# The k-v products of a linear attention, two heads at once or each head in its own 64 columns of the array

## The chip, the cores and the metric

The kernel runs on one core of one Trainium2 chip. The core has a matrix engine (TensorE, PE in the profile, with its weight loads shown apart as PEld), a vector engine (VectorE, DVE), a scalar engine (ScalarE, ACT), GpSimd (POOL), and SyncE (SP), which here only issues transfers. The metric is device time in microseconds for one execution; less is better. Three runs of the kernel before took 1629.92, 1631.16 and 1631.63 us, so its time is 1631.16 us (median).

## The reference

Inputs are q, k and v of shape (8, 8, 576, 64): batch, heads, sequence, head dimension, all float32. Then come two MLPs on 4608 tokens with 512 features and 2048 hidden units.

```
q_s = exp(q - max(q, -1)) / (sum over the head dimension + 1e-9)
k_s = exp(k - max(k, 2))  / (sum over the sequence + 1e-9)
kv  = einsum('bhsd,bhse->bhde', k_s, v)         # 64 x 64 for each head
x   = einsum('bhsd,bhde->bhse', q_s, kv)        # -> 4608 x 512
h = x @ w_in1;  g = max(0.01 h, h);     x = g @ w_out1
h = x @ w_in2;  g = h * sigmoid(h);     out = g @ w_out2
```

The change concerns the third line alone, the product of k_s and v over the 576 tokens of a sequence. The kernel multiplies exp(k) with v and with a column of ones, so that the same product gives the sum of exp(k) that k_s is divided by.

## The kernel before, in words

The work is cut into units: one unit is a pair of heads of one batch element for k and v, and a pair of heads of one block of 512 tokens for q. There are 36 units for q (9 blocks, 4 pairs) and 32 for k and v (8 batch elements, 4 pairs). Three generators do a unit: `k_task` (maximum over the sequence, exp, the kv product, scaling), `v_task` (the transfers of v) and `q_task` (softmax of q, its transposes, the product with kv).

For kv, the 576 tokens of the two heads lie in six sets of tiles that are used in turn. The first 512 tokens lie on 128 partitions, four to a partition (four chunks c), the last 64 on 64 partitions, as a fifth chunk. A chunk of exp(k) is 128 partitions x 128 columns (64 of each head); a chunk of v is 128 x 129: 64 columns of each head and a column of ones (`NV = 2 * D + 1`). Line 508 multiplies four chunks, line 509 the fifth, which has only 64 partitions; all five add up in one PSUM tile `pk`, 128 x 129. Only its two 64 x 64 diagonal blocks are kv of a head; the two other blocks mix the heads and are not read. On float32 operands the program's one matmul is two weight loads and two matmuls on the engine, so a unit's five matmuls are ten loads and ten passes.

Line 515 adds 1e-9 to the sum that stands in column 128 of `pk`, line 516 takes its reciprocal, and line 521 scales the two diagonal blocks into a zeroed 128 x 128 tile (`kvbuf`), which line 623 uses as weights for the product with q.

The order of the work of all engines is written out by a planner (`Queues`) from costs and ranks: the kv products of a unit are one step there, `op(("p", 1.1))`. In the stretch of the kv products PE otherwise does the first layer of the first MLP (lines 651 to 653: three products of split operands, 512 columns each), the transposes of k maxima and q (480, 486, 608) and line 623. The kv products are spread over the first 361 us; after that come the rest of layer one and the three other layers (lines 872 and 922). SP issues the transfers in one queue, in the planner's order. Before the first unit, POOL writes the columns of ones (line 980) and zeroes `kvbuf` (line 982).

Of the kernel before, what the change touches and what calls it, by code (L numbers as in the profile page):

```python
# [13 lines left out]
ACTF = mybir.ActivationFunctionType  # L14
# [12 lines left out]
def v_tt(n):  # L27
    return 0.16 + n / 960
# [6 lines left out]
def a_(n):  # L35
    return 0.19 + n / 1200
# [14 lines left out]
def op(*engines):  # L51
    return "op", engines


def wait(*keys):
    return "wait", keys


def get(ring):
    return "get", ring  # L60


class Queues:
# [14 lines left out]
    def spawn(self, rank, gen):  # L78
        self.tasks.append([rank, next(self.count), self.now, gen, None, 0.0, None])
        self.tasks.sort(key=lambda t: t[:2])  # L80
        self.step(next(t for t in self.tasks if t[3] is gen), None)
# [8 lines left out]
    def done(self, key):  # L90
        self.events[key] = self.now
# [111 lines left out]
def linear_attention_two_mlps(  # L203
# [24 lines left out]
    nc = tc.nc  # L228
    B, H, S, D = q.shape
    NT, DM = out.shape  # L230
    DFF = w_in1.shape[1]
    P = 128
# [6 lines left out]
    SR = S - SM  # L239
    EPS = 1e-9  # L240
# [21 lines left out]
    gd = [tc.dram_tile([NG, 4, P, TB], F32, name=f"gd{j}") for j in range(NB)]  # L262

    NKV = 8
    NV = 2 * D + 1
    ident = const.tile([P, P], F32, name="ident")
    ones = const.tile([P, 1], F32, name="ones")
    kvbuf = [const.tile([P, P], F32, name=f"kv{i}") for i in range(NKV)]
# [35 lines left out]
    def w_room(n, shape, dt, name):  # L304

        return wp.tile(shape, dt, tag=f"s{n}", name=f"{name}{n}")
# [43 lines left out]
    def split1(f):  # L350

        room = NW - NF + f
        raw = w_room(room, [P, 2 * DM], U32, "rw")
        yield from load_bits(raw, 0, 0, f)
        t = yield get(r_o)
        yield from decode(raw, t, DM)
        w = w_room(room, [P, 2, DM], F32R, "w")
        wtiles[f] = w
        yield op(("A", a_(DM)))
        copy("A", w[:, 0], t)  # L360
        yield op(("V", v_tt(DM)))
        sub("V", w[:, 1], t, w[:, 0])
        r_o.put(t)
        done(("w", f))
# [70 lines left out]
    sets = []  # L435
    for n in range(6):
        k_, v_ = (w_room(2 * n + i, [P, 2 * DM], F32, "u") for i in range(2))
        sets.append((k_[:, 0:640], v_[:, 0:5 * NV]))
    r_kv = Slots(qs, sets)
    r_q = Slots(qs)  # L440
    for n in range(3):
        t = gp.tile([P, 2, TB], F32, tag=f"g{n}", name=f"uq{n}")
        r_q.add(t[:, 0], t[:, 1])

    def k_task(n):

        b, j, p = units[n]
        if n >= NU:
            yield wait(("kvs", n - NU))
        of[n] = yield get(r_kv)  # L450
        kf, vv = of[n]
        done(("set", n))
        heads = slice(2 * p, 2 * p + 2)

        yield op(("D", 0.73))
        nc.sync.dma_start(
            out=kf[:, 0:512].rearrange("p (h c) -> p h c", h=2),
            in_=k[b, heads, 0:SM, :].rearrange("h (p c) d -> p h (c d)", c=4),
        )
        kh = kf[:, 0:512].rearrange("p (h c d) -> p h c d", c=4, h=2)  # L460
        k4 = kf[:, 0:512].rearrange("p (h c d) -> p c h d", c=4, h=2)
        yield op(("D", 0.56))
        k1 = kf[0:SR, 512:640]
        nc.sync.dma_start(
            out=k1.rearrange("p (h d) -> p h d", h=2), in_=k[b, heads, SM:S, :].rearrange("h p d -> p h d")
        )
        m1 = yield get(r_m)
        m2 = yield get(r_o)
        m2v = m2[:, 0:4 * D].rearrange("p (h c d) -> p h c d", h=2, c=2)
        yield op(("V", v_tt(256)))  # L470
        nc.vector.tensor_tensor(out=m2v, in0=kh[:, :, 0:2], in1=kh[:, :, 2:4], op=ALU.max)
        yield op(("V", v_tt(128)))
        nc.vector.tensor_tensor(out=m1, in0=m2v[:, :, 0], in1=m2v[:, :, 1], op=ALU.max)
        r_o.put(m2)
        m1f = m1.rearrange("p h d -> p (h d)")
        yield op(("V", v_tt(128)))
        nc.vector.tensor_tensor(out=m1f[0:SR], in0=m1f[0:SR], in1=k1, op=ALU.max)
        pm = yield get(r_attn)
        yield op(("p", 0.12))
        nc.tensor.transpose(pm[:, 0:P], m1f, ident)  # L480
        r_m.put(m1)
        nm = small[n % NU]["k"][:, 0:1]
        yield op(("V", v_tt(128)))
        nc.vector.tensor_reduce(out=nm, in_=pm[:, 0:P], axis=AX.X, op=ALU.max, negate=True)
        yield op(("p", 0.12))
        nc.tensor.transpose(pm[:, P:2 * P], nm.to_broadcast([P, P]), ident)
        nb = pm[:, P:2 * P]
        yield op(("V", v_tt(512)))
        nc.vector.tensor_tensor(
            out=k4, in0=k4,  # L490
            in1=nb.rearrange("p (h d) -> p h d", h=2).unsqueeze(1).to_broadcast([P, 4, 2, D]), op=ALU.add,
        )
        yield op(("V", v_tt(128)))
        nc.vector.tensor_tensor(out=k1, in0=k1, in1=nb[0:SR], op=ALU.add)
        r_attn.put(pm)
        kx = yield get(r_kx)
        yield op(("A", a_(512)))
        nc.scalar.activation(
            out=kx.rearrange("p (c h d) -> p c h d", c=4, h=2), in_=k4, func=ACTF.Exp
        )  # L500
        yield op(("A", a_(128)))
        nc.scalar.activation(out=k1, in_=k1, func=ACTF.Exp)
        yield wait(("v", n), *([("xm", n - NKV + NP)] if n >= NKV - NP else []))
        vv = vv.rearrange("p (c n) -> p c n", c=5)
        pk = yield get(r_attn)
        yield op(("p", 1.1))
        for c in range(4):
            nc.tensor.matmul(pk[:, 0:NV], lhsT=kx[:, c * P:(c + 1) * P], rhs=vv[:, c, :], start=c == 0, stop=False)  # L508
        nc.tensor.matmul(pk[:, 0:NV], lhsT=k1, rhs=vv[0:SR, 4, :], start=False, stop=True)  # L509
        r_kv.put(of.pop(n))  # L510
        r_kx.put(kx)
        done(("kv", n))
        rk = small[n % NU]["k"][:, 1:2]
        yield op(("V", 0.15))
        nc.vector.tensor_scalar_add(rk, pk[:, 2 * D:NV], EPS)
        nc.vector.reciprocal(out=rk, in_=rk)
        w = kvbuf[(b * NP + p) % NKV]
        for i in range(2):
            o = slice(i * D, (i + 1) * D)
            yield op(("A", a_(64)))  # L520
            nc.scalar.activation(out=w[o, o], in_=pk[o, o], func=ACTF.Copy, scale=rk[o])
        kv[b, p] = w
        r_attn.put(pk)
        done(("kvs", n))

    def v_task(n):
        b, j, p = units[n]
        yield wait(("set", n))
        t = of[n][1]
        t = t.rearrange("p (c n) -> p c n", c=5)  # L530
        for i in range(2):
            yield op(("D", 0.73))
            nc.sync.dma_start(
                out=t[:, 0:4, i * D:(i + 1) * D],
                in_=v[b, 2 * p + i, 0:SM, :].rearrange("(p c) d -> p c d", c=4),
            )

            yield wait()
        yield op(("D", 0.56))
        nc.sync.dma_start(  # L540
            out=t[0:SR, 4, 0:2 * D].rearrange("p (h d) -> p h d", h=2),
            in_=v[b, 2 * p:2 * p + 2, SM:S, :].rearrange("h p d -> p h d"),
        )
        yield wait()
        done(("v", n))
# [423 lines left out]
    def step(j, f):  # L969
        return place[j, f]  # L970
# [4 lines left out]
    with tc.manual_schedule():  # L975
        nc.vector.memset(ones, 1.0)
        make_identity(nc, ident)
        nc.scalar.activation(out=small[0]["k"][:, 0:1], in_=ones, func=ACTF.Exp)
        for _, t in sets:
            nc.gpsimd.memset(t.rearrange("p (c n) -> p c n", c=5)[:, :, 2 * D:], 1.0)  # L980
        for t in kvbuf:
            nc.gpsimd.memset(t, 0.0)

        for n in range(NP):
            r = -40 + 5 * n
            spawn(r, k_task(n))
            spawn(r + 1, q_task(n))
            spawn(r + 5, v_task(n))
        for n in range(NP, len(units)):
            b, j, p = units[n]  # L990
            r = -12 + 3 * p if j == 1 else step(j, 0) - 14 + 4 * p
            if b is not None:
                spawn(r, k_task(n))
                spawn(r, v_task(n))
            spawn(r, q_task(n))
        for f in range(NF):
            spawn(-36 + 6 * f if f < 4 else step(0, f) - 4, split1(f))
            if f < NH:
                spawn(f, layer0(0, f))
        spawn(0, layer0_all())  # L1000
        for t in (convert1, convert2, convert3):
            spawn(1000, t())
        spawn(0, later())
        for i in range(NG):
            for l in (1, 2, 3):
                spawn(step2(l, 0, i) - 8, weights(l, i))
        spawn(step2(1, 0, 0) - 4, g_all(1))
        spawn(step2(2, 0, 0) - 5, x_all())
        spawn(step2(3, 0, 0) - 4, g_all(3))
        spawn(step2(1, 0, 0), layers())  # L1010
        qs.run()
# [30 lines left out]
```

## Time and profile before

| | |
|---|---|
| median of three runs | 1631.16 us |
| the profiled execution | 1635.08 us |
| its span, first to last instruction | 1633.1 us |
| PE busy | 1603.1 us, 98% |
| PEld busy | 1501.8 us, 92% |
| DVE / ACT / POOL busy | 1194.2 / 851.3 / 39.1 us |
| share of L508 and L509 in PE's busy time | 37.1 + 16.4 us |
| mean granted TensorE clock | 0.995 |

The profile counts a matmul as busy from when it starts to when its last result is out, and the next one starts before that, so the busy times of a run of matmuls overlap. How long a pass holds the engine is read from the distance of two starts, not from its own duration. In a row of the timeline the first number is a start, the second the time from there to the end of the last instruction of the row, and x8 says that eight instructions are merged.

### The profile page before, as it was taken

What the parts mean: (1) busy time and instruction counts of PE and PEld (TensorE: products, weight loads), DVE (VectorE), ACT (ScalarE), POOL (GpSimd) and SP (SyncE); (2) the same over time, 40 slices, a digit from 0 to 9 for tenths busy, and PEclk for the clock granted to TensorE, in tenths of its full rate; (3) what the DMA queues carried; (4) which work ended last, traced back from release to release, by engine and by line L of the source; (5) the groups of instructions that cost most, each with busy time, mean ns of one, the idle gap of its engine ahead of it and who ended that gap; (6) DMA issues with size and microseconds to landing.
All of it is one profiled execution on the core that took longest, in us unless ns stands there. A gap on an engine that the chain in (4) does not pass through costs nothing.

```text
span 1633.1 us, 30896 instructions
## 1 busy us (share of the span) xinstructions
PE 1603.1 (98%) x11456; PEld 1501.8 (92%) x11456; DVE 1194.2 (73%) x2205; ACT 851.3 (52%) x1824; POOL 39.1 (2%) x53
## 2 busy tenths in 40 slices
PE   6899999999999999999999999999999999999999
PEld 4688888888788999999999999999999999999999
DVE  8886656657566887777788966666669877777775
ACT  5768756766445544444447433444446544444442
POOL 2101001000000000000000000000000000000000
PEclk9899999999999999999999999999999999999999
DMA  8766767777779655454558344333338544444442
GB/s 227 234 195 167 209 196 240 212 242 230 225 235 311 214 150 168 141 170 145 166 143 277 131 152 140 131 133 133 135 130 279 163 131 135 133 130 136 134 132 78
DMA packets 251030, 287.25 MB, mean 176 GB/s; under 512 B 59392, under 2 KB 182272, under 8 KB 250880
## 3 DMA queue, kind: packets, MB, share of 16 engines
q1 hardware_dynamic: 250880, 285.29, 56.6%
q8 instruction: 90, 1.47, 0.4%
q14 instruction: 60, 0.49, 0.1%
HBM read 168.82 MB, written 116.39 MB: 175 GB/s over the span
## 4 chain that ended last, share of the span: by engine, by line
PE 93%; DVE 5%; DMA 1%; issue 0%; ACT 0%; SPq 0%; DVEq 0%; ACTq 0%
PE b L922 22%; PE h L922 21%; PE b L872 11%; PE h L872 11%; PE h L651 8%; PE h L653 8%; PE h L652 8%; PE a L623 2%; PE a L508 2%; PE a L608 1%; DVE o L810 1%; PE a L509 1%; DVE a L292 1%; DVE x L292 1%; DVE g L292 0%
## 5 line engine op out<-in xcount | busy, mean ns | idle before, releaser
L651 PE MATMUL h<-x,w 128*128 128x512 f32 x576 | 238.5, 414 | 2.3 <-ACT w L296 1.6
L296 ACT ACTIVATE x<-x 128x512 fp32r<-128x512 f32 x209 | 131.8, 631 | 205.8 <-DMA x<-gda 91.0
L653 PE MATMUL h<-x,w 128*128 128x512 f32 x576 | 225.9, 392 | 1.2 <-DVE w L292 1.2
L652 PE MATMUL h<-x,w 128*128 128x512 f32 x576 | 225.4, 391 | 0.8 <-DVE x L292 0.5
L810 DVE TENSOR_TENSOR o<-o,b 128x512 f32<-128x512 f32 x190 | 128.1, 685 | 72.5 <-PE b L872 39.7
L810 DVE TENSOR_TENSOR o<-o,h 128x512 f32<-128x512 f32 x188 | 126.6, 685 | 62.7 <-PE h L872 36.7
L884 ACT ACTIVATE o<-o 128x512 f32<-128x512 f32 x144 | 89.2, 629 | 145.5 <-DVE o L810 144.7
L684 ACT ACTIVATE o<-h 128x512 f32<-128x512 f32 x144 | 85.9, 597 | 118.0 <-PE h L653 109.0
L296 ACT ACTIVATE x<-o 128x512 fp32r<-128x512 f32 x169 | 105.2, 631 | 70.0 <-DVE o L810 53.8
L922 PE MATMUL b<-a,x 128*128 128x256 f32 x1080 | 141.4, 283 | 0.1
L292 DVE TENSOR_TENSOR x<-x 128x512 fp32r<-128x512 f32 x209 | 137.2, 684 | 2.5
L651 PEld LDWEIGHTS h<-x,w 128*128 128x128 f32 x576 | 108.8, 189 | 29.2 <-ACT w L296 2.5
L922 PEld LDWEIGHTS b<-a,x 128*128 128x128 f32 x1080 | 134.7, 192 | 0.3 <-DVE x L292 0.3
L922 PE MATMUL b<-x,a 128*128 128x256 f32 x1044 | 132.0, 284 | 0.6 <-DVE x L292 0.5
L653 PEld LDWEIGHTS h<-x,w 128*128 128x128 f32 x576 | 108.4, 188 | 25.6 <-DVE w L292 2.3
L872 PE MATMUL h<-x,a 128*128 128x256 f32 x1008 | 130.0, 283 | 1.3 <-DVE x L292 1.3
L652 PEld LDWEIGHTS h<-x,w 128*128 128x128 f32 x576 | 108.9, 189 | 22.8 <-issue 1.2
L922 PEld LDWEIGHTS b<-x,a 128*128 128x128 f32 x1044 | 128.1, 192 | 1.1 <-DVE x L292 1.0
L872 PEld LDWEIGHTS h<-x,a 128*128 128x128 f32 x1008 | 124.9, 192 | 1.5 <-DVE x L292 1.5
L922 PE MATMUL h<-x,a 128*128 128x256 f32 x996 | 126.0, 283 | 0.2
L872 PE MATMUL b<-x,a 128*128 128x256 f32 x960 | 123.8, 283 | 1.3 <-DVE x L292 1.3
L922 PEld LDWEIGHTS h<-x,a 128*128 128x128 f32 x996 | 122.3, 192 | 0.7 <-DVE x L292 0.6
(116 smaller groups left out, 2819.3 us busy)
## 6 DMA issues: line engine op xcount, KB each, us to landing
gda<-o SPq DMA_DIRECT2D x144, 256.0 KB, 2.6
gd<-o SPq DMA_DIRECT2D x144, 256.0 KB, 2.6
x<-gd SPq DMA_DIRECT2D x102, 256.0 KB, 2.7
x<-gda SPq DMA_DIRECT2D x89, 256.0 KB, 2.8
a<-wc SPq DMA_DIRECT2D x84, 256.0 KB, 4.3
wc<-o SPq DMA_DIRECT2D x72, 256.0 KB, 3.2
raw<-in_moe_w_out_dram SPq DMA_DIRECT2D x32, 512.0 KB, 4.2
g<-gda SPq DMA_DIRECT2D x37, 256.0 KB, 2.7
```

The costliest lines, as they stand in the source:

```text
L292: engines[e].tensor_tensor(out=out_, in0=a, in1=b.bitcast(F32), op=ALU.subtract)
L296: nc.scalar.activation(out=out_, in_=in_, func=ACTF.Copy)
L508: nc.tensor.matmul(pk[:, 0:NV], lhsT=kx[:, c * P:(c + 1) * P], rhs=vv[:, c, :], start=c == 0, stop=False)
L623: nc.tensor.matmul(po, lhsT=kv[bb, p], rhs=qT.rearrange("p (c t) -> p c t", c=4)[:, :, a:e], start=True, stop=True)
L651: nc.tensor.matmul(h, lhsT=w[:, 0, kk], rhs=x[:, 0], start=kk == 0, stop=False)
L652: nc.tensor.matmul(h, lhsT=w[:, 0, kk], rhs=x[:, 1], start=False, stop=False)
L653: nc.tensor.matmul(h, lhsT=w[:, 1, kk], rhs=x[:, 0], start=False, stop=kk == KD - 1)
L684: nc.scalar.activation(out=o, in_=h, func=ACTF.Prelu, alpha=0.01)
L810: nc.vector.tensor_tensor(out=o, in0=a, in1=b, op=alu)
L872: nc.tensor.matmul(bank[:, r * HB:(r + 1) * HB], lhsT=w4[:, a, r, k], rhs=x3[:, b, k], start=n == 0, stop=n == 5,)
L884: nc.scalar.activation(out=t, in_=t, func=ACTF.Silu)
L922: nc.tensor.matmul(bank[:, m * HB:(m + 1) * HB], lhsT=s[:, a, at:at + P], rhs=x[:, b, r * HB:(r + 1) * HB], start=i + m + n == 0, stop=i = ...
```

## The change

Each of the five chunks is multiplied head by head: the weights are the 64 columns of exp(k) of one head, the moving operand the 64 columns of v of that head and a column of ones of its own (65), and the result goes to that head's 64 partitions of `pk`, columns 0 to 64. So five matmuls of 128 x 129 become ten of 64 x 65, and the built program marks them as 128 x 64 parts of the array, at columns 0 and 64 in turn. The mixed blocks are no longer computed. The fifth chunk now has 128 partitions, the upper 64 of them zero in both k and v; POOL writes these zeros once, at the start. Three transfers of v have other destinations, the sum is read from column 64, and line 521 reads columns 0 to 63 for both heads.

```
-    NV = 2 * D + 1
+    NV = 2 * (D + 1)
...
-        for c in range(4):
-            nc.tensor.matmul(pk[:, 0:NV], lhsT=kx[:, c * P:(c + 1) * P], rhs=vv[:, c, :], start=c == 0, stop=False)
-        nc.tensor.matmul(pk[:, 0:NV], lhsT=k1, rhs=vv[0:SR, 4, :], start=False, stop=True)
+        for c in range(5):
+            kc = kx[:, c * P:(c + 1) * P] if c < 4 else kf[:, 512:640]
+            for h in range(2):
+                o = slice(h * D, (h + 1) * D)
+                nc.tensor.matmul(
+                    pk[o, 0:D + 1], lhsT=kc[:, o], rhs=vv[:, c, h * (D + 1):(h + 1) * (D + 1)],
+                    start=c == 0, stop=c == 4,
+                )
...
-        nc.vector.tensor_scalar_add(rk, pk[:, 2 * D:NV], EPS)
+        nc.vector.tensor_scalar_add(rk, pk[:, D:D + 1], EPS)
...
-            nc.scalar.activation(out=w[o, o], in_=pk[o, o], func=ACTF.Copy, scale=rk[o])
+            nc.scalar.activation(out=w[o, o], in_=pk[o, 0:D], func=ACTF.Copy, scale=rk[o])
...
-                out=t[:, 0:4, i * D:(i + 1) * D],
+                out=t[:, 0:4, i * (D + 1):i * (D + 1) + D],
...
-            out=t[0:SR, 4, 0:2 * D].rearrange("p (h d) -> p h d", h=2),
+            out=t[0:SR, 4].rearrange("p (h d) -> p h d", h=2)[:, :, 0:D],
...
-        for _, t in sets:
-            nc.gpsimd.memset(t.rearrange("p (c n) -> p c n", c=5)[:, :, 2 * D:], 1.0)
+        for t_, t in sets:
+            t5 = t.rearrange("p (c h d) -> p c h d", c=5, h=2)
+            nc.gpsimd.memset(t5[:, :, :, D:], 1.0)
+
+            nc.gpsimd.memset(t_[SR:P, 512:640], 0.0)
+            nc.gpsimd.memset(t5[SR:P, 4, :, 0:D], 0.0)
```

The order of the work on the engines stays what it was: apart from line numbers, PE, DVE, ACT and SP have the same sequence, but for the kv products themselves. On PE, around the last unit (u is a set's tile of k or v, kx the exp of the first 512 tokens, a the PSUM tile pk, h and w the first layer), before:

```order
L653 MATMUL h<-x_126,w_713 128x512
L508 MATMUL a<-u_173,kx 128x129 x4
L509 MATMUL a<-u_173,u_172 128x129
L651 MATMUL h<-x_123,w_742 128x512
L652 MATMUL h<-x_123,w_742 128x512
```

and now:

```order
L659 MATMUL h<-x_126,w_765 128x512
L512 MATMUL a<-u_173,kx 64x65 x8
L512 MATMUL a<-u_173,u_172 64x65 x2
L657 MATMUL h<-x_123,w_794 128x512
L658 MATMUL h<-x_123,w_794 128x512
```

Ten matmuls of half the columns on both sides stand in the place of five; nothing else moved. On SP, at the start of the program, with what each transfer waits for (DMAHW are other transfers), before:

```order
L319 DMA rw_207<-in_moe_w_in_dram 128x4x256
L533 DMA u_171<-in_v_dram 128x4x64
L456 DMA u_172<-in_k_dram 128x2x256
L464 DMA u_172<-in_k_dram 64x2x64
L563 DMA uq_182<-in_q_dram 128x2x256
L533 DMA u_173<-in_v_dram 128x4x64 [waits DMAHW0_49]
L456 DMA u_174<-in_k_dram 128x2x256 [waits DMAHW1_49]
L533 DMA u_171<-in_v_dram 128x4x64 [waits DMAHW4_49,DMAHW2_49]
```

and now:

```order
L319 DMA rw_219<-in_moe_w_in_dram 128x4x256
L539 DMA u_171<-in_v_dram 128x4x64 [waits Pool_49]
L456 DMA u_172<-in_k_dram 128x2x256
L464 DMA u_172<-in_k_dram 64x2x64
L569 DMA uq_182<-in_q_dram 128x2x256
L539 DMA u_173<-in_v_dram 128x4x64 [waits DMAHW0_49,Pool_49]
L456 DMA u_174<-in_k_dram 128x2x256 [waits DMAHW1_49]
L539 DMA u_171<-in_v_dram 128x4x64 [waits DMAHW2_49]
```

The first transfer of v into each set now waits for POOL's writes to that set, and the second head's transfer no longer waits for the first head's (DMAHW4).

## Rows read from the trace of the kernel before

**Rows 1.** The page's head: span, then busy time, share and instructions by engine.

```profile
span 1633.1 us, 30896 instructions
PE 1603.1 (98%) x11456; PEld 1501.8 (92%) x11456; DVE 1194.2 (73%) x2205; ACT 851.3 (52%) x1824; POOL 39.1 (2%) x53
```

**Rows 2.** Busy time by stretch: length, PE, PEld, DVE, ACT, POOL, clock, DMA.

```profile
0.00:25.00 25.00, 11.57 (x40) 8.32 (x41) 17.68 (x41) 11.76 (x22) 7.24 (x25) 1.00 0.86 242
25.00:50.00 25.00, 21.21 (x101) 14.80 (x99) 24.45 (x59) 15.10 (x33) 8.09 (x7) 1.00 0.65 179
50.00:70.00 20.00, 16.51 (x62) 11.13 (x63) 15.97 (x44) 15.96 (x36) 4.50 (x4) 0.70 0.95 301
...
110.00:230.00 120.00, 120.00 (x608) 98.05 (x606) 74.93 (x218) 86.95 (x326) 9.90 (x10) 1.00 0.63 183
230.00:365.00 135.00, 135.00 (x667) 111.11 (x666) 86.96 (x221) 94.90 (x308) 5.97 (x5) 1.00 0.75 231
```

**Rows 3.** The chain that ended last, by line: 111 to 360 us, then 0 to 70.

```profile
by line: PE h L651 25.2%; PE h L653 24.6%; PE h L652 24.4%; PE a L508 8.3%; PE a L623 7.3%; PE a L608 4.3%; PE a L509 3.8%; PE a L486 1.1%; PE a L480 1.0%
...
by line: DMA gda<-o 7.0%; PE a L508 6.9%; PE a L623 6.0%; DMA rw<-in_moe_w_in_dram 5.8%; DVE o L340 5.5%; DVE w L292 4.7%; DVE rq L583 4.3%; DVE u L489 4.3%; DVE o L331 3.6%; DVE o L471 3.6%; DVE x L292 3.1%; issue 2.9%; DVE m L473 2.8%; DV
```

**Rows 4.** L508 alone by stretch: length, PE (instructions), PEld, clock, DMA.

```profile
110.00:230.00 120.00, 12.67 (x96) 12.25 (x96) 1.00 0.63 183
230.00:365.00 135.00, 12.78 (x96) 11.88 (x96) 1.00 0.75 231
```

**Rows 5.** Timeline of PE at the last unit: start, us, engine, line, operation.

```profile
359.65 0.39 PE L653 MATMUL h<-x,w 128*128 128x512 f32 x1
359.88 1.05 PE L508 MATMUL a<-u,kx 128*128 128x129 f32 x8
360.86 0.49 PE L509 MATMUL a<-u,u 64*128 64x129 f32 x2
361.28 0.50 PE L651 MATMUL h<-x,w 128*128 128x512 f32 x1
361.61 0.39 PE L652 MATMUL h<-x,w 128*128 128x512 f32 x1
```

**Rows 6.** The same, only the first pass of L508 and the last of L509.

```profile
359.88 0.27 PE L508 MATMUL a<-u,kx 128*128 128x129 f32 x1
...
361.08 0.27 PE L509 MATMUL a<-u,u 64*128 64x129 f32 x1
```

**Rows 7.** Weight loads (PEld) of L509 and L651 there; then all of L509's.

```profile
360.86 0.29 PEld L509 LDWEIGHTS a<-u,u 64*128 64x128 f32 x2
361.28 0.19 PEld L651 LDWEIGHTS h<-x,w 128*128 128x128 f32 x1
...
L509 PEld LDWEIGHTS a<-u,u x64: 182/186/336, 15.9 to 361.0; 64*128 64x128 f32 x64
```

**Rows 8.** Timeline of PE at two products of line 623, of 64 and 128 columns.

```profile
396.28 0.33 PE L623 MATMUL a<-uq,kv 128*128 128x64 f32 x2
396.74 0.39 PE L652 MATMUL h<-x,w 128*128 128x512 f32 x1
...
341.18 0.38 PE L623 MATMUL a<-uq,kv 128*128 128x128 f32 x2
341.63 0.39 PE L652 MATMUL h<-x,w 128*128 128x512 f32 x1
```

**Rows 9.** Timeline of POOL, and of SP's issues, at the start.

```profile
1.44 1.19 POOL L982 MEMSET kv<- 128x128 f32 x8
5.90 1.04 POOL L577 TENSOR_TENSOR uq<-uq,q 128x512 f32<-128x512 f32 x1 [3.27 <-DVE q L572]
...
3.15 0.58 SPq L533 DMA_DIRECT2D u<-in_v_dram  x1
```

**Rows 10.** Waits: who for whom, us in total, times, longest; SP's in 0 to 365 us.

```profile
DVE k L515 <- PE a L509: 18.8, 23, 1.9
SPq L533 <- DMA u<-in_v_dram: 5.1, 7, 1.5
```

## The prediction

> **What bounds the kernel now.** I read the page's head first: PE is busy for 1603.1 of 1633.1 us, DVE for 73% [rows 1]. Then the stretches in which the kv products stand. From 110 to 365 us PE is busy for the whole length of both stretches, and DVE and ACT for 62 to 72% [rows 2]. Up to 70 us it is otherwise: PE is busy for 49 of 70 us, DVE for 24.45 of the 25 us in the middle. The chain of work that ended last says the same: from 111 to 360 us its parts are PE alone, 8.3% of it L508 and 3.8% L509; up to 70 us it goes over transfers, DVE and PE, and L508 has 6.9%, which is 4.8 us [rows 3]. L508 has 192 engine instructions after 110 us, at eight to a unit 24 of the 32 units [rows 4]. So 24 units lie where a microsecond of PE is a microsecond of the end, and eight where it is that only in part.
>
> Next the timeline at one unit, read by distances of starts. In the last unit, L508 starts at 359.88; the eight passes take 1.05 and one takes 0.27 [rows 5, 6], so seven distances make 0.78, and a pass holds the engine 0.111 us. L651 starts at 361.28 and L652 at 361.61; an undisturbed pass of 512 columns takes 0.23 (359.65 to 359.88) [rows 5]. The unit costs 361.61 - 359.88 - 0.23 = 1.50 us.
>
> Where do they go? Eight passes of L508 are 0.89. The last of them starts at 359.88 + 0.78 = 360.66 and would hand on at 360.77, but L509's load starts at 360.86: 0.09 of nothing. L509's loads are two, of 0.29 together and 0.186 for one [rows 7], so the second starts at 360.97; L509's second pass starts at 361.08 [rows 6]. Its first load is not hidden (0.11), then come two passes of 0.11 each to 361.19. The load of L651 starts at 361.28: again 0.09 of nothing, then an unhidden load (L652 comes 0.33 after L651 instead of 0.23: 0.10). The sum is 0.89 + 0.09 + 0.11 + 0.22 + 0.09 + 0.10 = 1.50. So going to another form of the array (64 rows here) and back costs 0.39 us, whatever is done there.
>
> What holds a pass of 0.11? Line 623 shows it. A product of 64 columns takes from 396.28 to L652 at 396.74, 0.46, and one of 128 columns from 341.18 to 341.63, 0.45 [rows 8]. Less L651's 0.23, two passes take 0.22 to 0.23 in both: half the columns gain nothing while the weights are 128 columns wide. A load of 128 columns thus takes 0.11 as well, and the next pass's load runs beside the present pass.
>
> **The change, part by part.** *Switches.* Two remain, now from 128 x 128 to 128 x 64 at the unit's start and back at its end. The nearest row is L509's: 0.09 each, an unhidden load in (half as wide, 0.055) and out (0.10): 0.34 us, 0.05 less than before.
>
> *Passes.* Twenty stand in the place of ten, each with 65 columns instead of 129 (0.111 x 65 / 129 = 0.056) and a load of 64 instead of 128 columns (0.055). No row shows two halves of the array at work, so the pace of these passes is bounded from both sides:
> - below, both halves at once. The order is two passes of head 0, two of head 1, and so on; the two of one head follow each other, the second of one can run with the first of the other. That makes 11 steps of 0.056: 0.62 us. The unit costs 0.34 + 0.62 = 0.96, 0.54 less.
> - in the middle, one pass after another with hidden loads: 20 x 0.056 = 1.12, the unit 1.46, 0.04 less. With 0.002 us more to a pass it is 1.50, nothing.
> - above, one after another with loads that aren't hidden, or loads that cost 0.11 at half the width too: 20 x 0.111 = 2.22, the unit 2.56, 1.06 more.
>
> I take the lower end. The rows show that the array loads weights for one product while it streams another, as long as these don't need the same cells; the two heads share neither columns nor partitions of the result. The nearest measured row, L509 in its 64-row form, keeps load and pass side by side but has a single part to work with, so it says nothing against two. The estimate is weaker than the rest of the sum, and the range keeps all three.
>
> A rule of the Trainium skill speaks against this. In L509 the second load starts 0.11 after the first, at 360.97, when the first pass has just begun, and the second pass follows 0.22 after the first load's start [rows 6, 7]: load and pass ran together, though both use the same 64 rows. "TensorE: Matmul & The Clock Gate", Part 3 (The mechanism), states that in packed tiles a load overlaps with running matmuls only when its row group differs. Both heads use all rows here, so by that rule no load is hidden, and the unit costs the 2.56 us of the upper bound. The trace contradicts it for a load within one tile. The same section gives three column tiles 2.38 times the speed of one; no run here shows that, and at that rate the unit would come out near the lower bound.
>
> *The 24 later units:* 24 x 0.54 = 13.0 us. *The eight early ones:* of the 4.8 us of L508 on the chain half could go, 2.4, if nothing else were late; but there DVE's work and transfers stand beside it on the chain, and the next of them takes over. Between 0 and 2.4 I take 1.2. The clock was 0.70 from 50 to 70 us (12 of 20 us at the 1.2 GHz level) with PE busy for 16.51 of 20 [rows 2]; a shift there can move such a stretch, which I hold at 3 us either way, in the range only.
>
> *What follows kv.* DVE waits for L509 in 23 units, 18.8 us in total [rows 10]; that wait gets shorter, and DVE isn't the bound after 70 us. L515 and L521 read as many elements as before.
>
> *POOL's zeros.* Twelve writes are added ahead of the zeroing of kvbuf, whose eight take 1.19, 0.15 each: 1.8 us. POOL ended at 2.63 and would end at 4.4; its next work starts at 5.90 after 3.27 of idleness for DVE [rows 9]. Cost nothing, with 1.5 us to spare; beyond that they would delay the first softmax of q one for one. The first transfer of v waits for POOL's first three writes, but is issued only at 3.15, when they are long done; behind it SP's whole queue would wait, k of the next unit first. The second transfer of each unit loses its wait for the first: SP lost 5.1 us to that in 7 cases [rows 10], most of it early; whoever is next in that queue waits for something else, so I count 0.
>
> Sum: 13.0 + 1.2 = 14.2 us less. The profiled execution took 1635.08, so 1620.9; it lies 3.9 above the median of the runs, 1631.16, which makes **1617.0**.
>
> **The rivals.**
> - *The halves take turns.* The change then doesn't do what it says: the halves exist, but each works while the other rests. For it: no row shows two passes of one time, each of L508 starts 0.111 after the one before; and loads, which can be no less than 0.055 each, would take 20 x 0.055 = 1.1 us if only one runs at a time. Against it: the two halves need nothing of each other. The time is 0 to 1 us less: 1630 to 1631.
> - *The loads come into the open* (slower). Load, pass, load, pass within a half, and no load of the other half beside a pass. For it: at each switch of form the load was in the open (0.11 and 0.10); if going from one half to the other is treated like that, it happens in every pass. Against it: L509's second load. The price is 24 x 1.06 = 25.4 and about half of 8 x 1.06 early, together 30 us: 1661. It decides from where a pass with its load takes over 0.065 us: then 24 x (0.34 + 20 x 0.065 - 1.50) = 3.3 us, the bound below.
> - *The early stretch eats it.* The later units save 13, and a moved cold stretch of the clock costs 3: 1621, inside the forecast's own range.
>
> **How the numbers follow.** The forecast has 0.46 (its own range 1611 to 1626, with steps of 0.05 to 0.065 us and the early units at either end), the halves in turn 0.26, loads in the open, wholly or in part, 0.28 (1635 to 1665, most near the upper end of it only if all are open). A measurement of this kernel tells 0.2%, 3.3 us, from no change. Faster: 0.46 and a little of the second case, 0.48; within: 0.24; slower: 0.28. The range that leaves 2 in 10 out is 1611 to 1648: some 0.07 lies below and 0.13 above.
>
> **What would show it.** In the profile after, the starts in one unit: from the first kv pass to the next product some 0.85 us instead of 1.40 (361.28 - 359.88) if the forecast is right, 1.4 if the halves take turns, 2.4 if loads are open. Loads of head 1 must start while a pass of head 0 runs, and passes of different heads must lie less than 0.056 apart on average. PE must stay busy throughout from 110 to 365 us, and the first layer must end about 13 us earlier; if it does and the end doesn't move, a later transfer was the bound and the sum was wrong. POOL's zeros must end before 5.90.

## The result, and the profile after

The changed kernel takes 1617.4 us (median of six runs, 1616.68 to 1619.66) against 1631.1 us before (six runs): a ratio of 0.9916, 95% interval 0.9900 to 0.9931. The forecast was 1617.0 us. The profiled execution took 1616.68 us.

The page's head, to be read beside [rows 1]:

```profile
span 1614.9 us, 31515 instructions
PE 1581.0 (98%) x11776; PEld 1478.7 (92%) x11776; DVE 1192.2 (74%) x2205; ACT 850.1 (53%) x1824; POOL 41.9 (3%) x65
```

PE has 320 matmuls more (32 units, ten passes more each) and is busy for 22 us less; the other engines have the same work, POOL twelve instructions more. What the change did stands in one unit. The timeline of PE at the last unit, as [rows 5] showed it before (L657 to L659 are the first layer's three lines, L512 the kv products):

```profile
342.34 0.39 PE L659 MATMUL h<-x,w 128*128 128x512 f32 x1
342.66 0.69 PE L512 MATMUL a<-u,kx 128*64 128x65 f32 x16
343.18 0.29 PE L512 MATMUL a<-u,u 128*64 128x65 f32 x4
343.39 0.50 PE L657 MATMUL h<-x,w 128*128 128x512 f32 x1
343.73 0.39 PE L658 MATMUL h<-x,w 128*128 128x512 f32 x1
```

From the last pass of the first layer ahead of the unit (342.34) to the second one behind it (343.73) there are 1.39 us, of which two passes of 512 columns are 0.46: the unit costs 0.93. Before, the same two distances were 361.61 - 359.65 = 1.96, less 0.46: 1.50 [rows 5]. Sixteen passes, on two halves eight steps, take from 342.66 to 343.18, 0.52; the first load, in the open, is some 0.055 of that, which leaves 0.058 for a step of two passes. That the two of a step run together is seen where the timeline is cut just behind the first pass, and then a little later:

```profile
342.66 0.27 PE L512 MATMUL a<-u,kx 128*64 128x65 f32 x1
...
342.66 0.28 PE L512 MATMUL a<-u,kx 128*64 128x65 f32 x2
```

One pass lasts 0.27 from start to last result, two last 0.28: they start 0.01 apart. The loads, of which [rows 7] showed those of L509 before:

```profile
342.66 0.55 PEld L512 LDWEIGHTS a<-u,kx 128*64 128x64 f32 x16 [0.35 <-issue]
343.12 0.20 PEld L512 LDWEIGHTS a<-u,u 128*64 128x64 f32 x4
343.39 0.19 PEld L657 LDWEIGHTS h<-x,w 128*128 128x128 f32 x1
```

The sixteen loads of 64 columns lie in the same 0.69 us as the sixteen passes, so loads run beside passes. The switches are those of [rows 5 to 7]: L512's first load starts 0.32 after the start of a pass that holds the engine for 0.23, 0.09 late; L658 again comes 0.34 after L657 instead of 0.23.

DVE's wait for the kv products, the first of [rows 10], is down from 18.8 us to 5.1 (L521 is now the addition that was L515):

```profile
DVE k L521 <- PE a L512: 5.1, 12, 1.1
```

And POOL at the start, against [rows 9] (the last of its eighteen writes to the sets, the zeroing of kvbuf, and its first work on q):

```profile
4.48 0.20 POOL L990 MEMSET u<- 64x128 f32 x1
4.74 1.23 POOL L992 MEMSET kv<- 128x128 f32 x8
5.94 1.03 POOL L583 TENSOR_TENSOR uq<-uq,q 128x512 f32<-128x512 f32 x1
```

The idle 3.27 us ahead of POOL's first work on q are used up, and L583 starts at 5.94 instead of 5.90.

In the stretch of the later units PE is still busy throughout, as in [rows 2]:

```profile
108.00:230.00 122.00, 122.00 (x822) 97.87 (x822) 80.04 (x237) 94.40 (x344) 9.63 (x9) 1.00 0.68 198
230.00:348.00 118.00, 118.00 (x688) 95.78 (x687) 78.79 (x200) 85.30 (x286) 5.91 (x5) 1.00 0.79 241
```

### The profile page after: what moved, and what is told of

Its sections match the earlier page's. It is cut to its first block, busy times and chain, and to the rows that moved or that the text cites. A ratio compares the mean times of both kernels' runs of the same rounds, so it can differ in the third digit from the quotient of the medians.

```text
span 1614.9 us, 31515 instructions
## 1 busy us (share of the span) xinstructions
PE 1581.0 (98%) x11776; PEld 1478.7 (92%) x11776; DVE 1192.2 (74%) x2205; ACT 850.1 (53%) x1824; POOL 41.9 (3%) x65
## 3 DMA queue, kind: packets, MB, share of 16 engines
q8 instruction: 92, 1.51, 0.4%
## 4 chain that ended last, share of the span: by engine, by line
PE 94%; DVE 5%; DMA 1%; ACT 0%; issue 0%; SPq 0%; DVEq 0%; ACTq 0%
PE b L928 22%; PE h L928 22%; PE b L878 11%; PE h L878 11%; PE h L657 8%; PE h L659 8%; PE h L658 8%; PE a L629 2%; PE a L512 1%; PE a L614 1%; DVE x L292 1%; DVE o L816 1%; DVE a L292 1%; DMA rw<-in_moe_w_in_dram 1%; DVE g L292 0%
## 5 line engine op out<-in xcount | busy, mean ns | idle before, releaser
L657 PE MATMUL h<-x,w 128*128 128x512 f32 x576 | 237.5, 412 | 3.8 <-ACT w L296 3.1
L659 PE MATMUL h<-x,w 128*128 128x512 f32 x576 | 225.5, 392 | 1.2 <-DVE w L292 1.2
L658 PE MATMUL h<-x,w 128*128 128x512 f32 x576 | 224.8, 390 | 1.1 <-DVE x L292 1.1
L657 PEld LDWEIGHTS h<-x,w 128*128 128x128 f32 x576 | 108.4, 188 | 30.1 <-ACT w L296 3.9
L659 PEld LDWEIGHTS h<-x,w 128*128 128x128 f32 x576 | 108.1, 188 | 25.9 <-DVE w L292 2.8
L658 PEld LDWEIGHTS h<-x,w 128*128 128x128 f32 x576 | 108.5, 188 | 23.2 <-DVE x L292 1.7
```

The source lines that it names most:

```text
L657: nc.tensor.matmul(h, lhsT=w[:, 0, kk], rhs=x[:, 0], start=kk == 0, stop=False)
L658: nc.tensor.matmul(h, lhsT=w[:, 0, kk], rhs=x[:, 1], start=False, stop=False)
L659: nc.tensor.matmul(h, lhsT=w[:, 1, kk], rhs=x[:, 0], start=False, stop=kk == KD - 1)
```

## The experiments

All ratios are to the kernel before, run on the same chip in the same group of runs. "Unit" is worked out as above, from the profile's last unit (in plan_cost from the last one that stands between passes of 512 columns). In the code, "..." marks lines that are left out.

| kernel | median us | ratio, 95% interval | unit, us |
|---|---|---|---|
| before | 1631.1 to 1634.3 by group | 1 | 1.50 |
| after | 1617.40 | 0.9916, 0.9900 to 0.9931 | 0.93 |
| after, second group | 1616.87 | 0.9901, 0.9887 to 0.9915 | 0.93 |
| by_head | 1625.47 | 0.9953, 0.9939 to 0.9967 | 1.32 |
| pad_only | 1621.29 | 0.9929, 0.9917 to 0.9942 | 1.11 |
| halves_unpadded | 1621.35 | 0.9924, 0.9911 to 0.9938 | 1.07 |
| twice | 1631.80 | 0.9991, 0.9982 to 1.0001 | 1.51 |
| same_half | 1631.60 | 0.9999, 0.9989 to 1.0010 | 1.50 |
| early_twice | 1616.47 | 0.9905, 0.9888 to 0.9922 | 0.93 |
| plan_cost | 1616.47 | 0.9899, 0.9883 to 0.9916 | 0.93 |
| by_two | 1618.39 | 0.9907, 0.9890 to 0.9923 | 0.98 |

**Both heads in the same half** (same_half). It asks whether the two halves of the columns are what gains, or just narrow passes.

```
-                o = slice(h * D, (h + 1) * D)
+                o, at = slice(h * D, (h + 1) * D), h * P
...
-                    pk[o, 0:D + 1], lhsT=kc[:, o], rhs=vv[:, c, h * (D + 1):(h + 1) * (D + 1)],
+                    pk[0:D, at:at + D + 1], lhsT=kc[:, o], rhs=vv[:, c, h * (D + 1):(h + 1) * (D + 1)],
...
```

> The changed kernel, but both heads' products go to the same 64 partitions of the sum, that is to columns 0 to 63 of the array; head 1 lies in the sum's columns 128 to 192, and 32 small additions on DVE are done in two pieces. Same matmuls, same order. Theory (two halves of the columns work side by side): nothing can overlap, 20 passes of 0.058 us, a unit costs 0.34 + 1.15 = 1.49 us instead of 0.93, 13.4 us more than the changed kernel, the time of before within 2 us. Rival (narrow passes are just short, 0.029 us each, whatever columns they use): the time of the changed kernel within 2 us.

Measured: 1631.60 us, the time of before. The timeline of PE at its last unit:

```profile
355.87 0.39 PE L660 MATMUL h<-x,w 128*128 128x512 f32 x1
356.18 1.15 PE L512 MATMUL a<-u,kx 128*64 128x65 f32 x16
357.17 0.40 PE L512 MATMUL a<-u,u 128*64 128x65 f32 x4
357.49 0.50 PE L658 MATMUL h<-x,w 128*128 128x512 f32 x1
357.83 0.39 PE L659 MATMUL h<-x,w 128*128 128x512 f32 x1
```

Sixteen passes take 0.99 us instead of 0.52, 0.058 for each after the first load of 0.055. The same matmuls, of the same size, in the same order: when both heads use the same columns, all of the gain is gone. This is the plainest of the runs, and it is also what the rival "the halves take turns" would have looked like: 0.058 for a pass, its load hidden. The columns of the array and the 64 partitions of the sum change together here, so no run tells which of the two the heads must not share.

**The heads one after the other** (by_head), and **two chunks at a time** (by_two). They ask whether the halves overlap only where the program lets their passes alternate.

```
-        for c in range(5):
-            kc = kx[:, c * P:(c + 1) * P] if c < 4 else kf[:, 512:640]
-            for h in range(2):
+        for h in range(2):
+            for c in range(5):
+                kc = kx[:, c * P:(c + 1) * P] if c < 4 else kf[:, 512:640]
```

> The changed kernel with the ten kv matmuls of a unit in another order: five of head 0, then five of head 1. Theory (the halves run side by side, but only where the program lets a pass of one head follow one of the other): hardly anything can overlap now, 20 passes of 0.056 to 0.058 us one after another, a unit costs 0.34 + 1.15 = 1.49 us and the time is 1629 to 1633 us, that of the kernel before. Rival (the gain is that of the fifth chunk's padding, the order of the heads is nothing): 1616 to 1619 us, as with the heads in turn.

Measured: 1625.47 us, between the two. In the timeline of its last unit, kx are the first four chunks of either head, and u the fifth:

```profile
354.28 0.39 PE L659 MATMUL h<-x,w 128*128 128x512 f32 x1
354.59 0.73 PE L512 MATMUL a<-u,kx 128*64 128x65 f32 x10
355.11 0.22 PE L512 MATMUL a<-u,u 128*64 128x65 f32 x1
355.17 0.22 PE L512 MATMUL a<-u,kx 128*64 128x65 f32 x1
355.17 0.22 PE L512 MATMUL a<-u,u 128*64 128x65 f32 x1
355.23 0.45 PE L512 MATMUL a<-u,kx 128*64 128x65 f32 x5
355.52 0.28 PE L512 MATMUL a<-u,u 128*64 128x65 f32 x2
355.73 0.50 PE L657 MATMUL h<-x,w 128*128 128x512 f32 x1
356.06 0.39 PE L658 MATMUL h<-x,w 128*128 128x512 f32 x1
```

Head 0 has eight passes on kx and then two on u. Ahead of its first on u, at 355.11, ten passes on kx have started: two of them are head 1's, though the program has them behind head 0's two on u. So a pass can start ahead of passes of the other half that stand before it in the program, and my theory, that nothing would overlap, was wrong; the rival, that order is nothing, was wrong as well. But the lead is short: L657 comes 1.14 after the first pass, where the changed kernel has 0.73 and same_half, without any overlap, 1.31. That is three of the ten steps that the changed kernel saves; most passes of either head ran alone.

The order with two chunks of a head at a time (four passes) was run for that:

```
-        for c in range(5):
+        for g in ((0, 1), (2, 3), (4,)):
+            for h, c in [(h, c) for h in range(2) for c in g]:
```

> The changed kernel with two chunks of head 0, then two of head 1, then the next two of each, then the fifth chunk of each: four passes of a half stand together, where the changed kernel has two and the order by heads ten. Theory (a half that is free takes up its next pass while at most three passes of the other half stand ahead of it): the halves lag each other by one step at each change, at most 0.058 us five times, from the first to the last pass 0.64 to 0.87 us instead of 0.58 (changed kernel) and 0.98 (by heads); 1618 to 1624 us. Rival (passes of both halves run together only where they are neighbours in the program): over 0.87 us and over 1624 us.

```profile
343.26 0.39 PE L659 MATMUL h<-x,w 128*128 128x512 f32 x1
343.58 0.73 PE L512 MATMUL a<-u,kx 128*64 128x65 f32 x16
344.10 0.34 PE L512 MATMUL a<-u,u 128*64 128x65 f32 x4
344.37 0.50 PE L657 MATMUL h<-x,w 128*128 128x512 f32 x1
344.70 0.39 PE L658 MATMUL h<-x,w 128*128 128x512 f32 x1
```

Measured: L657 comes 0.79 after the first pass (0.73 in the changed kernel), one step of 0.06 lost in the whole unit, the least that I expected (0.64 from the first to the last pass); 1618.39 us. With runs of four passes of one half nearly all of the overlap is there, with runs of ten most of it is gone.

**Padding alone** (pad_only) and **halves alone** (halves_unpadded). They share out the gain.

```
-        nc.tensor.matmul(pk[:, 0:NV], lhsT=k1, rhs=vv[0:SR, 4, :], start=False, stop=True)
+        nc.tensor.matmul(pk[:, 0:NV], lhsT=kf[:, 512:640], rhs=vv[:, 4, :], start=False, stop=True)
...
```

> The kernel before, but with the fifth chunk of k and v padded with zeros to 128 partitions: five matmuls of 128 x 129 without the 64-row form, no halves. Theory (switches and halves both count): ten passes of 0.111 us and no switch, a unit costs 1.11 us instead of 1.50 before and 0.93 after, 24 x 0.39 = 9.4 us less than before: 1620 to 1623 us. Rival (all of the gain is the padding): 1616 to 1619 us. Rival (all of the gain is the halves): 1629 to 1633 us.

```profile
348.30 0.39 PE L653 MATMUL h<-x,w 128*128 128x512 f32 x1
348.53 1.05 PE L508 MATMUL a<-u,kx 128*128 128x129 f32 x8
349.42 0.39 PE L509 MATMUL a<-u,u 128*128 128x129 f32 x2
349.56 0.48 PE L651 MATMUL h<-x,w 128*128 128x512 f32 x1
349.87 0.40 PE L652 MATMUL h<-x,w 128*128 128x512 f32 x1
```

Measured: 1621.29 us, as the theory had it. No pass here comes late: L509 follows L508 after 0.89, eight passes of 0.111, where before it took 0.98 [rows 5]. The two passes over the fifth chunk take no longer with zeros on 64 partitions, 0.11 each, and both switches are saved: 0.39 us a unit, two thirds of the change's gain, without any halves.

```
-            kc = kx[:, c * P:(c + 1) * P] if c < 4 else kf[:, 512:640]
+            kc, m = (kx[:, c * P:(c + 1) * P], P) if c < 4 else (k1, SR)
...
-                    pk[o, 0:D + 1], lhsT=kc[:, o], rhs=vv[:, c, h * (D + 1):(h + 1) * (D + 1)],
+                    pk[o, 0:D + 1], lhsT=kc[:, o], rhs=vv[0:m, c, h * (D + 1):(h + 1) * (D + 1)],
...
```

> The changed kernel without the padding: the fifth chunk is multiplied on its 64 partitions, head by head, in 64 x 64 parts of the array, and the zeros are not written. Theory: the halves still run side by side, but each unit has a third switch of form, 0.09 us of nothing and an unhidden load of 0.055: 0.15 us more for a unit, 24 x 0.15 = 3.6 us, 1620 to 1623 us. Rival (padding is what gains): 1628 to 1633 us.

```profile
344.20 0.39 PE L659 MATMUL h<-x,w 128*128 128x512 f32 x1
344.52 0.69 PE L512 MATMUL a<-u,kx 128*64 128x65 f32 x16
345.13 0.33 PE L512 MATMUL a<-u,u 64*64 64x65 f32 x4
345.40 0.50 PE L657 MATMUL h<-x,w 128*128 128x512 f32 x1
345.73 0.39 PE L658 MATMUL h<-x,w 128*128 128x512 f32 x1
```

Measured: 1621.35 us, again as expected. The fifth chunk starts 0.61 after the first pass instead of 0.52: the third switch. So neither part does the whole; padding without halves leaves 1.11, halves without padding 1.07, both 0.93. On top of the padding the halves win only 0.18: the passes take 0.58 instead of 1.11, but two switches, 0.35 together, come back with them.

**The products twice** (twice), and **twice in the first eight units alone** (early_twice, whose edit is shown; in the other, R is 2 for all units).

```
-        for c in range(5):
+        R = 2 if n < 8 else 1
+        for r, c in [(r, c) for r in range(R) for c in range(5)]:
...
```

> The changed kernel with the ten kv matmuls of a unit done twice into the same sum (sum and products double alike). Theory (a step of two passes is 0.058 us and PE's time is the end's time after 70 us): 0.58 us more for a unit, 24 x 0.58 = 13.9 us in the later units and up to 4.6 in the eight early ones: 1631 to 1636 us. Rival (PE has slack behind which passes hide): under 1625 us. Rival (the first passes after a switch are the cheap ones, later ones 0.11): over 1640 us.

> The changed kernel with the ten kv matmuls done twice in the first eight units alone (sum and products double alike). It prices the part of the program before 70 us, where PE isn't alone on the chain. Theory of the prediction (a quarter of that PE time reaches the end): 8 x 0.58 x 0.25 = 1.2 us more than the changed kernel, 0 to 2.4. Rival (all of it does): 4.6 us more. Rival (the stretch at the 1.2 GHz level between 50 and 72 us goes away when PE has more work there): up to 3 us less.

Measured: 1631.80 and 1616.47 us. With all units doubled, the last unit stands between these two rows, and the time is that of before:

```profile
355.39 0.39 PE L659 MATMUL h<-x,w 128*128 128x512 f32 x1
...
357.36 0.39 PE L658 MATMUL h<-x,w 128*128 128x512 f32 x1
```

The unit costs 357.36 - 355.39 - 0.46 = 1.51, as before the change: the way in which PE's time is spent doesn't matter, and in the later units it reaches the end in full.

In the early units alone, the median is no higher than the changed kernel's (1616.47 against 1616.87 in that group). That isn't yet to say that the doubled work costs nothing, for the five runs are of two kinds: three with a granted clock of 1.00 (1615.10 to 1616.47 us) and two with 0.998 and 0.996 (1618.94 and 1621.38). The ten runs of the changed kernel have 0.996 to 0.999, none 1.00; at 0.998 they took 1616.68 to 1617.57 us, at 0.996 1619.66. So at like clock the doubling costs some 1.7 us of the 4.6 that it adds. The trace, of the run with 0.998, has the first later unit at

```profile
109.75 0.69 PE L513 MATMUL a<-u,kx 128*64 128x65 f32 x16
```

and the changed kernel's two traces have it at 108.08 and 107.74, 1.7 and 2.0 earlier. So about 0.4 of the early PE time is on the path, somewhat more than the quarter of the theory. The last rival has something for it too: a granted clock of 1.00 means that the stretch at the 1.2 GHz level was missing in three of five runs, which would have paid the doubling back. Five runs are few, and whether the added work was the cause isn't shown.

**The planner's cost** (plan_cost).

```
-        yield op(("p", 1.1))
+        yield op(("p", 0.7))
```

> The changed kernel with the planner told that a unit's kv step costs 0.7 instead of 1.1, in the proportion of the measured 0.93 to 1.50 us. PE's work is the same in another order here and there. Theory (PE is the bound from 70 us on, whatever the order): the time of the changed kernel within 2 us. Rival (the old cost keeps other steps waiting): 2 to 5 us less.

Measured: 1616.47 us, no different from the changed kernel (1616.87): the old cost holds nothing up that can be measured. **The changed kernel again** (after_again) is the measure of that group:

> The changed kernel itself, beside the three others of this group on the same chip. All theories: ratio to before 0.990 to 0.993.

Measured: a ratio of 0.9901.

**Where the time went.** From the first of the later units to the last there are 23 units. Between the starts of these two, the traces have (plan_cost, with another order of the work, is left out):

| kernel | from, to | length, us | less than before | 23 x gain of a unit |
|---|---|---|---|---|
| before | 111.71, 359.88 | 248.17 | | |
| after | 108.08, 342.66 | 234.58 | 13.6 | 13.1 |
| after_again | 107.74, 342.32 | 234.58 | 13.6 | 13.1 |
| early_twice | 109.75, 345.48 | 235.73 | 12.4 | 13.1 |
| by_two | 108.06, 343.58 | 235.52 | 12.7 | 12.0 |
| halves_unpadded | 106.48, 344.52 | 238.04 | 10.1 | 9.9 |
| pad_only | 108.91, 348.53 | 239.62 | 8.6 | 9.0 |
| by_head | 111.06, 354.59 | 243.53 | 4.6 | 4.1 |
| same_half | 108.26, 356.18 | 247.92 | 0.3 | 0.0 |
| twice | 107.72, 355.71 | 247.99 | 0.2 | -0.2 |

So in each kernel this stretch gets shorter by what its units save, within 0.7 us. What else two traces differ by lies ahead of the first later unit or behind the last; for before and after that is 3.6 and 1.0 us.

## Why the prediction was right, point by point

*The bound.* Right: 24 later units times 1.50 - 0.93 = 0.57 are 13.7 us, and in the traces the stretch from the first to the last of them, 23 units long, is 13.6 us shorter. Doubled units give all of it back (twice).

*The price of a unit.* Predicted 0.96, measured 0.93. The switches were right to 0.01. The passes came in ten steps of 0.058, not eleven of 0.056: I took it that the second head's first pass would wait for the first head's second, as the program has it, and it doesn't.

*The choice between the bounds.* This was the weak step, told as such: no row before showed two halves at work. The reason given, that loads run beside passes as long as they don't need the same cells, isn't what the rows said: in L508 and L509 loads are hidden behind passes of the same cells, and that says nothing of two passes at a time. The lower bound was a guess that came true. The trace after shows two passes side by side, and same_half prices the middle bound that wasn't taken: 20 passes one after another, a unit of 1.50 against the 1.46 to 1.50 worked out, the time of before. The upper bound, loads in the open, came up nowhere; even within one half the loads are hidden. The Trainium skill's rule on packed tiles ("TensorE: Matmul & The Clock Gate", Part 3, The mechanism), that a load overlaps only with matmuls of another row group, doesn't hold here: all passes of a unit use all 128 rows, and 20 loads and 20 passes go through in ten steps of 0.058. The same section also has matmuls start in strict program order; by_head shows passes of one half start ahead of the other's that precede them.

*The early units.* The prediction has 1.2 us, between 0 and 2.4. early_twice doesn't refute this: 0.4 of the early PE time is 8 x 0.57 x 0.4 = 1.8 us at like clock, as an estimate. What the sum left out, and put in the range alone, is the stretch at the 1.2 GHz level: none of the changed kernel's ten runs has a granted clock of 1.00, while 12 of 39 runs of the kernel before have, in the groups where its clock is on record. The early units are also not all as cheap as the last one. In the first of them, before the change, L508's eight passes take 1.93 us instead of 1.05, though [rows 2] has a clock of 1.00 there:

```profile
14.08 1.93 PE L508 MATMUL a<-u,kx 128*128 128x129 f32 x8
```

*The sum.* 14.2 us were predicted; the medians lie 13.7 apart in the first group and 15.7 in the second. That 1617.0 and 1617.4 are so close is partly luck: the medians of before alone differ by 3.2 us between groups.

*The signs named ahead.* From the first kv pass to the next product it is 0.73 us; the 0.85 named doesn't follow from the prediction's own terms, which give 0.055 + 0.62 + 0.09 = 0.77. PE stays busy throughout the stretch. The first layer's last product starts 17.9 us earlier (531.9 and 514.0), not 13, because 3.6 of this stood before the first later unit.

*POOL.* The writes were mis-sized: 1.8 us predicted, 3.3 measured (kvbuf is zeroed from 4.74 on instead of 1.44 [rows 9]). The eighteen writes come in sets of three that take 0.58 us each (starts at 1.25, 1.42, 1.56, and the next set's first at 1.82), where 0.15 for each of twelve had been counted. L583 is late by 0.04 us only, but of the 1.5 us to spare nothing is left; by this pace one more set would have delayed the first softmax of q.

*What isn't settled.* Beyond the unit's price, differences of some 2 us remain. Single executions carry stretches at the 1.2 GHz level between 50 and 72 us, where PE is busy for three quarters of the time: in one group the runs of before with a granted clock of 1.00 took 1630.0 to 1631.4 us, those of 0.996 and 0.997 1634.0 to 1636.4. Which run has such a stretch varies from run to run of one kernel, and the medians of groups differ by that. Taken at a clock of 0.999 or 1.00 alone, before has 1630.6 and pad_only 1621.3, 9.3 apart, which is 24 x 0.39; by_head has 1624.5, 6.1 less, where its units give only 24 x 0.18 = 4.3, and halves_unpadded has one such run, 1618.2, 12.4 less, where its units give 24 x 0.43 = 10.3. These 2 us don't lie in the later units, whose stretch is shorter by 4.6 and 10.1, as the units give. halves_unpadded reaches its first later unit at 106.48, the earliest of all traces, and both are some 1.4 us shorter than before behind the last one. What causes that stays open.

## What to carry to other kernels

Where the profile shows one engine busy throughout a stretch, price an edit by the distances between starts in that stretch, the gaps on both sides included: here 0.39 of 1.50 us were two changes of the array's form for a short last chunk, which zeros on the missing partitions avoid. Two products of 64 columns that share neither columns nor results went through the array in the time of one here, when they alternated in the program in short runs. And the same microsecond of PE was worth one in one stretch and less than half in another, so count units by stretch before multiplying, and compare runs of like clock before reading a small difference as nothing.

## What the runs showed of the hardware

- Two products of 64 columns each, in different halves of the array's columns, run side by side: 20 passes in ten steps of 0.058 us, and 0.058 for each pass when both use the same half.
- A pass can overtake passes of the other half that precede it in the program, but only a few of them: from a unit's first pass to the next product it takes 0.73 us with runs of two passes of one half, 0.79 with runs of four, 1.14 with runs of ten, and 1.31 where nothing can overlap.
- Going from 128 x 128 to 64 x 128 or 128 x 64, from there to 64 x 64, or back, cost about 0.09 us of nothing and an unhidden load each time (0.05 for a load of 64 columns, 0.10 to 0.11 for 128). Zeros up to 128 rows avoid the 64-row form: 0.39 of 1.50 us a unit.
